# Reordering the second tile of a fused retention and cosine-gated feed-forward kernel, and a k and v load held back in the third

## The chip, the cores and the metric

One core of a Trainium2 chip. The metric is the time of one execution of the kernel on the device, in microseconds (us); the time of a kernel is the median of its runs. The engines: TensorE (PE in the profile, its weight loads PEld), VectorE (DVE), ScalarE (ACT), GpSimd (POOL), and SyncE (SP), which here issues nearly all transfers between HBM and the on-chip memory. Each engine takes its instructions in the order in which the program gives them; waits between engines are semaphores.

## The reference

Retention over 8 batches, 8 heads, 576 positions and 64 features per head, then a feed-forward layer over the 4608 tokens:

```python
scores = scale * np.matmul(q, k.transpose(0, 1, 3, 2))
ret = scores * Dmat                     # gamma[h] ** (i - j) where i >= j, else 0
x = np.matmul(ret, v).transpose(0, 2, 1, 3).reshape(4608, 512)
h = x @ w_in                            # 512 -> 2048
out = (h * np.cos(h)) @ w_out           # 2048 -> 512
```

All inputs and the output are float32; the kernel rounds to bf16 ahead of the matmuls.

## The kernel before

**Blocks and tiles.** The 4608 tokens are 18 token blocks of 256 rows (0 to 17) and nine tiles of 512 tokens (0 to 8). Tile n of the feed-forward layer takes its x from blocks 2n and 2n+1. Retention runs ahead of the feed-forward work: while tile 1 is computed, blocks 3 to 6 are prepared, turned, scored or summed.

**What one block needs.** Its q, k and v are loaded by SP (`load`, L140 and L154). q and k are multiplied by powers of gamma (`scaled`, L203; mostly on POOL, for block 3's q on DVE) and v is rounded (`round_v`, L214, POOL). PE turns q and k (`turned`: 32 transposes, L239, into one PSUM bank or two), and two copies bring them back to SBUF as qkT, one on DVE and one on ACT (L245); where both halves lie in one bank, ACT's copy waits for DVE's. `scores` makes 32 small matmuls (L332), and DVE masks them in two instructions (L341, "ret"). `sums_of` makes the block's state sums (24 or 32 small matmuls, L365, banks "st"); its inner `add` chains them on DVE with the running state (up to four instructions, L412 and L416, "s_all"), and ACT rounds the result (L425, "sb"). `outputs` multiplies ret with v (L449) and the states with q (L477), and ACT copies the result to SBUF as xT (L496).

**The feed-forward half.** `mm1` computes h for a group of 1024 PSUM columns (L525), then a cosine on ACT (L538) and a product on DVE (L539) leave gT. Two cosine buffers alternate. Tile 0 multiplies gT with w_out directly (64 matmuls of 512 columns, L1046, in an order written out by hand, with a list `todo` of retention work at fixed places). From tile 1 on, the second product uses seven smaller products per tile instead of eight (`mm2_seven`, `product`, L640), which need sums of quarters of gT (`g_sum`, L579, on DVE and POOL) and sums of quarters of w_out, computed once (`w_sums`, L557, on DVE, four pieces of eight e's at a time; number 7 is written in place over a quarter of w_out). Sums, copies (L673) and stores (L656) of the results follow.

**Tile 1.** Its h is computed in eight groups of 16 matmuls of 256 columns, here called G0 to G7 (in the code the pairs (1, 0) to (1, 7)). G0 to G3 take the columns of block 2, G4 to G7 those of block 3. Each group fills one PSUM bank, in the order m, a, b, m, b, m, a, b, and a bank comes free when DVE has made the product of the group that filled it before. The table `inside` names what is put into a group: key 2 is the middle of a group, key 4 its end, for these groups of four parts. After G3 the product with number 1 is computed, with `outputs(3, "a")` inside it; G4 waits for the xT that this leaves. After G7 come the products 2, 4, 6, 5, 7 and 3, with `first_scores` ahead of 6 (scores and state sums of blocks 4 and 5, on the banks a, b and m), and the outputs of blocks 4 and 5 ahead of 7 and 3.

**Around the border of tile 0 and tile 1**, PE has in this order: the last output matmuls of tile 0, `outputs(2, "b")`, three more, the turn of block 3 on bank "a", the last one, G0. DVE has: the scaling of block 3's q (L203 two times, waiting for the load of q), the copy of tile 0's second output out of bank "m" (L1056), the copy of block 3's turn (L245), the copy of the fourth output (L1056), a piece of the weight sums 4 (L557), the masks of block 3. G0 writes bank "m".

**Order of transfers.** All loads and stores of tile 2 and of the later tiles are issued by SP in program order. `mm2_seven` makes a store for each quarter result (numbers s 0 to 3); `stored(s)` prepares the next block on POOL (`step`) and loads one further ahead (`load_next`). From tile 3 on some stores and loads are put off into lists (`late`) that run ahead of the products 4 and 3; a gate makes a transfer wait for the output matmul that was recorded last (`tiles["end"]`, L477).

Of the kernel before, what the change touches and what calls it, by code (L numbers as in the profile page):

```python
# [17 lines left out]
def kernel(  # L18
# [28 lines left out]
    last = NT - 1  # L47
# [444 lines left out]
    def outputs(j, bank, guard=None):  # L492
        ps = psum.tile([P, DG, BK], F32, tag=bank, name="ov")
        rest = out_own(j, ps, guard)
        out_carried(j, ps)
        nc.scalar.copy(x_of(j), ps)  # L496
        for run in rest:
            run()
# [47 lines left out]
    def w_sums(x, e0, e1):  # L546
        if x == 7:
            w_sum[x] = w_quarter(0, 1)
        elif x not in w_sum:
            w_sum[x] = consts.tile([P, E2, N2], BF16, tag=f"ws{x}", name=f"ws{x}")  # L550
        a, b = {
            5: lambda: (w_quarter(0, 1), w_quarter(0, 0)),
            6: lambda: (w_quarter(1, 1), w_sum[5]),
            4: lambda: (w_quarter(1, 0), w_sum[6]),
            7: lambda: (w_quarter(1, 1), w_quarter(0, 1)),
        }[x]()
        nc.vector.tensor_tensor(  # L557
            out=w_sum[x][:, e0:e1], in0=a[:, e0:e1], in1=b[:, e0:e1], op=ALU.subtract
        )
# [101 lines left out]
    def mm2_seven(n, at, stored, xs=(1, 2, 6, 4, 7, 5, 3), early=None):  # L661
        pend = []

        def flush():
            while pend:
                pend.pop(0)()

        def add(out_, in0, in1):
            return lambda: nc.vector.tensor_tensor(out=out_, in0=in0, in1=in1, op=ALU.add)  # L669

        def copied(tag, x):
            t = op.tile([P, 2, N2], F32, tag=tag, name="ot")
            held.append(lambda ps=tiles["all", x]: nc.scalar.copy(t, ps))  # L673
            return t

        late = {4: [], 3: []}

        def store(t, r, c, s):
            where = n * W + r * 256, c * N2, (c + 1) * N2, t

            def go():
                if 2 < n < last and s == 0:
                    stored_rows(*where, halves=(0,))
                    late[4].append(lambda: stored_rows(*where, halves=(1,), gate=tiles["end"]))
                    stored(s, late)
                elif 2 < n < last - 1 and s == 1:
                    late[3].append(lambda: stored_rows(*where))
                else:
                    queues = (nc.sync, nc.scalar) if n == last and s else (nc.sync, nc.sync)
                    stored_rows(*where, queues)  # L690
                    stored(s)

            return go

        def copies():
            while held:
                held.pop(0)()

        for x in xs:
            if x not in at:  # L700
                copies()
                flush()
            else:
                if at[x].__name__ in ("nothing", "first_scores", "last_outputs", "turning"):
                    copies()
                at[x](flush, pend)
                copies()
                for run in late.pop(x, ()):
                    run()
            if x == 6 and n > 1:  # L710
                late_sums(n, (3,))
            parts = product(n, x, early)
            if x == 1:
                c11 = copied("a", 1)
                tiles["c11"] = c11
                if n > 1:
                    late_sums(n, (5, 6))
            elif x == 2:
                c11 = tiles["c11"]
                if n == 1:  # L720
                    p2 = copied("d", 2)
                    continue
                pend[:0] = [add(c11, c11, tiles["all", 2]), store(c11, 0, 0, 0)]
            elif x == 6:
                u1 = copied("b", 1)
            elif x == 4:
                c21 = copied("c", 4)
            elif x == 7 and n == 1:
                pend += [
                    add(c21, c21, tiles["all", 1]),  # L730
                    add(c22, c22, tiles["all", 1]),
                    store(c21, 1, 0, 1),
                    store(c22, 1, 1, 2),
                    add(c11, c11, p2),
                    store(c11, 0, 0, 0),
                ]
            elif x == 7:
                c22 = copied("d", 1)
                pend += [add(c21, c21, tiles["all", 1]), store(c21, 1, 0, 1)]
            elif x == 5 and n == 1:  # L740
                c22 = copied("d", 5)
            elif x == 5 and n == last:
                for (j, c0, c1), ps in zip(parts, tiles["o", 5]):
                    pend.append(add(c22[:, j, c0:c1], ps, c22[:, j, c0:c1]))
                pend.append(store(c22, 1, 1, 2))
            elif x == 5:
                pend += [
                    add(c22, c22, tiles["all", 5]),
                    add(u1, u1, tiles["all", 5]),
                    store(c22, 1, 1, 2),  # L750
                ]
            elif n < last:
                pend += [add(u1, u1, tiles["all", 5 if n == 1 else 3]), store(u1, 0, 1, 3)]
                flush()
            else:
                flush()
                copies()
                for (j, c0, c1), ps in zip(parts, tiles["o", 5]):
                    add(u1[:, j, c0:c1], ps, u1[:, j, c0:c1])()
                    if c1 == N2:  # L760
                        stored_rows(
                            n * W + j * P, N2, DM, u1[:, j : j + 1, :], (nc.sync, nc.scalar)
                        )
# [3 lines left out]
    def load_next(**kw):  # L767
        nonlocal loaded
        if loaded < NB:
            load(loaded, **kw)  # L770
            loaded += 1

    def step(then_load=True):

        nonlocal prepared
        if prepared < NB:
            prep(prepared)
            round_v(prepared)
            prepared += 1
            if then_load:  # L780
                load_next()
# [184 lines left out]
    def states_and_scores(j, st_bank, sc_bank):  # L966
        add = sums_of(j, st_bank) if st_bank else None
        masks = scores(j, [sc_bank])
        if add:
            add()()  # L970
        for masked in masks:
            masked()
# [3 lines left out]
    for n in range(NT):  # L976
        blocks = blocks_of.get(n) or [(e + k * E2, 0, W) for e in range(0, E2, 2) for k in range(2)]
        for i, (et, c0, cw) in enumerate(blocks):
            inside = {
                (0, 0): {2: block1_outputs},  # L980
                (1, 0): {2: lambda: w_sums(4, 0, 4), 4: lambda: states_and_scores(3, None, ("n", "st"))},
                (1, 1): {4: lambda: adds.append(sums_of(3, ("n", "st"))())},
                (1, 3): {1: lambda: (adds.pop()(), w_sums(6, 4, E2), w_sums(4, 4, E2))},
                (1, 4): {2: lambda: turned(4, ("st", "a"), (act, vec))},
                (1, 7): {2: lambda: turned(5, "m")},
                (2, 0): {1: lambda: adds.append(sums_of(6, ("n", "st"))())},
                (2, 1): {1: lambda: adds.pop()()},
                (2, 5): {1: lambda: turned(7, ("n", "st"))},
            }.get((n, i), {})
            mm1(n, et, c0, cw, banks_of.get(n, turn_of(n) * 3)[i], inside)  # L990
            if (n, i) == (1, 0):
                step(False)
                load_next()
            if (n, i) == (1, 1):
                step(False)
                for r0, ot in stores[3:] + stores[:3]:
                    stored_rows(r0, 0, DM, ot)
                load_next()
                step()
            if (n, i) == (1, 3):  # L1000
                w_sums(7, 0, 4)
                w_sums(7, 4, E2)
                mm2_seven(1, {}, None, (1,), lambda: outputs(3, "a"))
            if n:
                sums_after(n, i)
            if n == 2 and i in (2, 4):
                for y in range(2):
                    scaled(nc.gpsimd, 8, "q" if i == 2 else "k", y)
            if (n, i) == (2, 6):
                round_v(8)  # L1010
                prepared = 9
                load_next()
                load_next()
        if n == 0:
# [6 lines left out]
                (20, lambda: scaled(nc.vector, 2, "q", 1)),  # L1021
                (42, lambda: turned(2, "ab", (act, vec))),
                (42, lambda: round_v(2)),
                (63, lambda: turned(3, "a", (vec, act))),
                (48, lambda: states_and_scores(2, "a", "b")),
                (49, lambda: prep(3, nc.vector)),
                (60, load_next),
# [146 lines left out]
```

## Time and profile before

| | |
|---|---|
| median of 3 runs | 291.77 us (291.66 to 292.05) |
| the profiled execution | 292.45 us, its span 290.7 us |
| TensorE clock granted | 1.00 |
| PE busy | 283.5 us of the span, DVE 218.9, ACT 170.6, POOL 147.1 |
| chain of work that ended last | PE 86%, DVE 7%, DMA 4%, issue 1% |
| transfers | 42.62 MB, 147 GB/s on average |

The span runs from the first to the last instruction on the core, the execution's own time holds what lies around it as well. In the timelines, a row is a run of like instructions of one engine: start, length, engine, line, operation, output and inputs, count, and in brackets how long the engine sat idle before it and what ended that. The length of a run ends with the modelled end of its last instruction, which for PE lies a little after the moment at which the next one could start. In the table of stretches a row gives a stretch of the span, its length, then busy time and instruction count of PE, PEld, DVE, ACT and POOL, the granted clock, the share of the DMA engines and their GB/s.

### The profile page before, as it was taken

To read this page: it belongs to the slowest core of one execution; us is meant where nothing else is said; L and a number is where in the kernel's file an instruction comes from. 1 tells how busy PE (TensorE), PEld (TensorE's weight loads), DVE (VectorE), ACT (ScalarE), POOL (GpSimd) and SP (SyncE) were. 2 spreads that over 40 slices of the span, in tenths; PEclk is the share of its full clock that TensorE was granted. 3 is DMA by queue.
4 is the path that set the end of the run, shared out by engine and by line. 5 is a ranking of instruction groups with operands and counts; after the bars stand their busy time and mean duration, and the time that the engine had idled before them with its cause. 6 is when DMAs were issued, how large, how long until landed. Compare 5 with 4: busy or idle time off the path is not lost.

```text
span 290.7 us, 10530 instructions
## 1 busy us (share of the span) xinstructions
PE 283.5 (97%) x4336; PEld 190.5 (66%) x4336; DVE 218.9 (75%) x309; ACT 170.6 (59%) x200; POOL 147.1 (51%) x169
## 2 busy tenths in 40 slices
PE   7999999999999999999999999999999999999994
PEld 2664446888854786468746874687458845874584
DVE  5777757998868876796779776986698669745943
ACT  6756216657577745677466737673767476536620
POOL 7940423887986994369235933494338023002400
PEclk9999999999999999999999999999999999999999
DMA  7999999988997999943794189417501130122013
GB/s 225 268 173 205 250 238 237 238 195 207 223 233 188 219 235 217 222 93 79 177 235 96 44 203 239 101 41 186 144 0 38 33 84 0 33 60 59 0 38 108
DMA packets 103853, 42.62 MB, mean 147 GB/s; under 512 B 68480, under 2 KB 103296, under 8 KB 103808
## 3 DMA queue, kind: packets, MB, share of 16 engines
q1 hardware_dynamic: 99104, 37.37, 52.8%
q0 software_dynamic: 4256, 4.19, 9.0%
q8 instruction: 36, 0.59, 0.9%
q10 hardware_dynamic: 448, 0.39, 0.4%
q14 instruction: 9, 0.07, 0.1%
HBM read 36.70 MB, written 9.44 MB: 159 GB/s over the span
## 4 chain that ended last, share of the span: by engine, by line
PE 86%; DVE 7%; DMA 4%; issue 1%; ACT 0%; DVEq 0%; ACTq 0%
PE h L525 40%; PE o L640 34%; PE o L1046 3%; PE tr L239 3%; DMA fq<-in_q_dram 3%; PE ov L449 3%; DVE gT L539 2%; DVE ret L312 1%; PE ov L477 1%; PE sc L332 1%; DMA fk<-in_k_dram 1%; PE st L365 1%; DVE qks L171 1%; DVE w_out_sb L557 1%; DVE ws L557 1%; DVE s_all L416 1%
## 5 line engine op out<-in xcount | busy, mean ns | idle before, releaser
L525 PE MATMUL h<-xT,w_in_sb 128*128 128x512 bf16 (+1 forms) x656 | 127.5, 353 | 0.3 <-DVE qkT L245 0.3
L539 DVE TENSOR_TENSOR gT<-h,cosh 128x1024 bf16<-128x1024 f32 x72 | 87.7, 1221 | 26.5 <-ACT cosh L538 25.4
L538 ACT ACTIVATE cosh<-h,half_pi 128x1024 f32<-128x1024 f32 x72 | 80.1, 1114 | 40.6 <-PE h L525 40.6
L525 PEld LDWEIGHTS <-w_in_sb 128*128 128x128 bf16 x656 | 63.6, 98 | 58.9 <-issue 0.5
L579 POOL TENSOR_TENSOR gs<-gT 128x512 bf16<-128x512 bf16 x30 | 38.1, 1271 | 98.9 <-DVE gT L539 98.2
L640 PEld LDWEIGHTS <-gs 128*128 128x128 bf16 x528 | 49.6, 98 | 5.9
L203 POOL TENSOR_TENSOR qks<-fk,gkc 128x512 bf16<-128x512 f32 x32 | 38.5, 1222 | 5.5 <-DMA fk<-in_k_dram 5.5
L640 PEld LDWEIGHTS <-gT 128*128 128x128 bf16 x384 | 36.6, 98 | 6.1
L669 DVE TENSOR_TENSOR ot<-ot,o 128x512 f32<-128x512 f32 x35 | 23.3, 682 | 20.8 <-ACT ot L673 11.0
L245 ACT COPY qkT<-tr 128x1024 bf16<-128x1024 bf16 x29 | 27.7, 1022 | 12.6 <-PE tr L239 11.0
L203 POOL TENSOR_TENSOR qks<-fq,gq 128x512 bf16<-128x512 f32 x28 | 31.5, 1146 | 4.8 <-DMA fq<-in_q_dram 4.3
L640 PE MATMUL o<-w_out_sb,gs 128*128 128x256 bf16 (+1 forms) x264 | 30.7, 270 | 0.0
L640 PE MATMUL o<-w_out_sb,gT 128*128 128x256 bf16 x256 | 30.6, 273 | 0.0
L640 PE MATMUL o<-ws,gs 128*128 128x256 bf16 (+1 forms) x264 | 30.4, 269 | 0.0
L673 ACT COPY ot<-o 128x512 f32<-128x512 f32 x33 | 19.2, 585 | 18.2 <-PE o L640 18.2
L341 DVE TENSOR_TENSOR ret<-sc,mask_c 128x512 bf16<-128x512 f32 x32 | 20.6, 683 | 7.0 <-PE sc L332 7.0
L214 POOL CAST vb<-fv 128x512 bf16<-128x512 f32 x35 | 21.4, 637 | 6.7 <-DMA fv<-in_v_dram 6.5
L425 ACT CAST sb<-s_all 128x768 bf16<-128x768 f32 (+2 forms) x17 | 15.6, 919 | 14.4 <-DVE s_all L416 14.4
L416 DVE TENSOR_TENSOR s_all<-st,s_all 128x256 f32<-128x256 f32 x49 | 20.7, 422 | 1.9 <-PE st L365 0.6
L496 ACT CAST xT<-ov 128x1024 bf16<-128x1024 f32 x16 | 16.2, 1012 | 8.3 <-PE ov L477 8.0
L579 DVE TENSOR_TENSOR gs<-gT 128x512 bf16<-128x512 bf16 (+1 forms) x24 | 16.0, 665 | 0.5
L640 PE MATMUL o<-ws,gT 128*128 128x256 bf16 x128 | 15.3, 273 | 0.0
(83 smaller groups left out, 212.1 us busy)
## 6 DMA issues: line engine op xcount, KB each, us to landing
out_dram<-ot SPq DMA_DIRECT2D x68, 128.0 KB, 2.5
fk<-in_k_dram SPq DMA_DIRECT2D x28, 256.0 KB, 5.3
fv<-in_v_dram SPq DMA_DIRECT2D x28, 256.0 KB, 4.1
fq<-in_q_dram SPq DMA_DIRECT2D x12, 512.0 KB, 5.2
w_out_sb<-in_moe_w_out_dram POOLq DMA_DIRECT2D x4, 512.0 KB, 9.7
fq<-in_q_dram SPq DMA_DIRECT2D x4, 384.0 KB, 5.9
fk<-in_k_dram SPq DMA_DIRECT2D x2, 512.0 KB, 6.0
fv<-in_v_dram SPq DMA_DIRECT2D x2, 512.0 KB, 5.9
```

The costliest lines, as they stand in the source:

```text
L203: return eng.tensor_tensor(out=dst.rearrange("p b a d -> p a b d"), in0=src.rearrange("p (a b) d -> p a b d", a=2), in1=by.rearrange("p (a ...
L214: runs[y](vb[:, y], f[:, :, y, :] if j < NP_B else f[:, y])
L245: lambda r=r: evacs[r](tiles["qkT", j][:, :, :, :, r * HP : r * HP + HP], pss[r])
L341: nc.vector.tensor_tensor(out=ret[:, he].rearrange("p b y i -> p (b y) i"), in0=ps[he].rearrange("p b y i -> p (b y) i"), in1=mask_c.unsqu ...
L416: nc.vector.tensor_tensor(out=s32[:, u], in0=ps[c.half][:, c.y], in1=s32[:, u - 1] if u else tiles["run"], op=ALU.add,)
L525: nc.tensor.matmul(ps[:, j, :], lhsT=w_in_sb[:, dg, (et + j) * P : (et + j + 1) * P], rhs=xT[:, dg, c0 : c0 + w], start=dg == 0 and not (i ...
L538: nc.scalar.activation(cosh, ps, ACTF.Sin, bias=half_pi, scale=1.0)
L539: nc.vector.tensor_mul(gT[:, et : et + m, c0 : c0 + w], ps, cosh)
L579: i = eng.tensor_tensor(out=tiles["gs", n, x][:, e : e + step], in0=a[:, e : e + step], in1=b[:, e : e + step], op=op_,)
L640: nc.tensor.matmul(dst[i], lhsT=lhs[:, e, j * P : (j + 1) * P], rhs=rhs[:, e, c0:c1], start=(fresh and e == 0 and (i == 0 or len(parts) > 2)),
L669: return lambda: nc.vector.tensor_tensor(out=out_, in0=in0, in1=in1, op=ALU.add)
L673: held.append(lambda ps=tiles["all", x]: nc.scalar.copy(t, ps))
```

## The change

No instruction is added or taken away on PE, DVE, ACT or POOL; they are put in another order, and two stores and a load change places on SP.

- Block 3's turn leaves the end of tile 0 and goes into the middle of G0, on bank "b" instead of "a". Its state sums go from the end of G1 to the end of G0, its scores from the end of G0 to the middle of G2. On DVE the copies of tile 0's outputs now stand together ahead of the copy of the turn, and the state additions ahead of the products of G0 and G1, the masks behind them.
- The two pieces of the weight sums 7 stood behind G3's product, ahead of DVE's copy of block 4's turn. Now the first piece stands behind this copy, and the second behind G5's product.
- In tile 2, the store with number 0 prepares a block and loads only q of the next (block 11); its k and v are put off to the place ahead of product 3, gated on the output matmul recorded last. There they stand behind the two stores of number 2, which come from product 5. The store with number 1 is put off in tile 2 as well, as it was from tile 3 on.

```diff
@@ mm2_seven, store @@
-                elif 2 < n < last - 1 and s == 1:
+                elif n == 2 and s == 0:
+                    stored_rows(*where)
+                    step(False)
+                    load(loaded, "q")
+                    late[3].append(lambda: load_next(names="kv", gate=tiles["end"]))
+                elif 1 < n < last - 1 and s == 1:
                     late[3].append(lambda: stored_rows(*where))
@@ the table inside @@
-                (1, 0): {2: lambda: w_sums(4, 0, 4), 4: lambda: states_and_scores(3, None, ("n", "st"))},
-                (1, 1): {4: lambda: adds.append(sums_of(3, ("n", "st"))())},
+                (1, 0): {
+                    2: lambda: (turned(3, "b", (vec, act)), w_sums(4, 0, 4)),
+                    4: lambda: adds.append(sums_of(3, ("n", "st"))()),
+                },
+                (1, 2): {2: lambda: states_and_scores(3, None, ("n", "st"))},
                 (1, 3): {1: lambda: (adds.pop()(), w_sums(6, 4, E2), w_sums(4, 4, E2))},
-                (1, 4): {2: lambda: turned(4, ("st", "a"), (act, vec))},
+                (1, 4): {2: lambda: (turned(4, ("st", "a"), (act, vec)), w_sums(7, 0, 4))},
@@ after a group @@
             if (n, i) == (1, 3):
-                w_sums(7, 0, 4)
+                mm2_seven(1, {}, None, (1,), lambda: outputs(3, "a"))
+            if (n, i) == (1, 5):
                 w_sums(7, 4, E2)
-                mm2_seven(1, {}, None, (1,), lambda: outputs(3, "a"))
@@ the list todo of tile 0 @@
-                (63, lambda: turned(3, "a", (vec, act))),
```

## The prediction

> **What bounds the kernel now.** I read the page's busy table first, then the table of stretches, then the chain of work that ended last, then each engine's timeline from 45 to 82 us, where the change lies.
>
> ```profile
> PE 283.5 (97%) x4336; PEld 190.5 (66%) x4336; DVE 218.9 (75%) x309; ACT 170.6 (59%) x200; POOL 147.1 (51%) x169
> ```
> ```profile
> 45.00:63.18 18.18, 17.22 (x353) 13.86 (x349) 16.64 (x22) 11.13 (x12) 12.77 (x14) 1.00 0.99 236
> 63.18:82.00 18.82, 18.67 (x434) 15.88 (x434) 16.41 (x24) 12.45 (x18) 15.46 (x15) 1.00 0.82 200
> 82.00:112.00 30.00, 30.00 (x530) 20.12 (x529) 23.70 (x32) 19.73 (x24) 25.70 (x27) 1.00 0.89 219
> ```
>
> First pair in each row: length, TensorE (PE) busy. From 82 us on PE has no hole until the tail, so whatever PE gains or loses before 82 us comes out whole at the end, and work moved after 82 us is free as long as PE does not have to wait for it. In 45 to 63.18 VectorE (DVE) is busy 16.64 of 18.18 us. Here are PE's two holes:
>
> ```profile
> 45.57 0.82 PE L1046 MATMUL o<-w_out_sb,gT 128*128 128x512 bf16 x3
> 46.49 0.29 PE L239 MATMUL tr<-ident,qks 64*128 64x64 bf16 x8
> 47.09 0.52 PE L239 MATMUL tr<-ident,qks 64*128 64x64 bf16 x24 [0.31 <-DVE qks L203]
> 47.55 0.39 PE L1046 MATMUL o<-w_out_sb,gT 128*128 128x512 bf16 x1
> ```
> ```profile
> 59.47 0.64 PE L239 MATMUL tr<-ident,qks 64*128 64x64 bf16 x32
> 60.04 2.79 PE L525 MATMUL h<-xT,w_in_sb 128*128 128x256 bf16 x24
> 63.18 0.49 PE L525 MATMUL h<-xT,w_in_sb 128*128 128x256 bf16 x3 [0.34 <-DVE qkT L245]
> ```
>
> A row ends about 0.16 after PE could take the next instruction (one matmul's latency over its pace). So hole one is 46.23 to 46.49 and 46.63 to 47.09, 0.72 in all: block 3's transposes wait for its q, scaled by DVE. Hole two: 24 matmuls at 0.109 (3.50 us for the 32 from 52.22) are done at 62.67; G6 starts at 63.18, 0.51 late, since its bank "a" waits for DVE's copy of block 4's turn. 1.23 us is all that can be won.
>
> **Part 1: block 3's turn into the middle of G0.** Hole one seems to go. But these rows decide what is late next:
>
> ```profile
> 45.74 1.29 DVE L203 TENSOR_TENSOR qks<-fq,gq 128x512 bf16<-128x512 f32 x2 [1.33 <-DMA fq<-in_q_dram]
> 46.95 0.68 DVE L1056 COPY ot<-o 128x512 f32<-128x512 f32 x1
> 47.66 0.69 DVE L245 COPY qkT<-tr 128x1024 bf16<-128x1024 bf16 x1
> ```
>
> G0 writes bank "m", which tile 0 still holds until DVE has copied its second output (L1056). That copy stands behind the same q scaling on DVE, and ends at 47.63. The built changed kernel keeps both the order on DVE and the wait of G0's first weight load on DVE. So G0 starts at 47.69 plus 0.03 instead of 47.77 (0.05 gained), PE now idle from 46.45, and the 32 transposes, which lay in that shadow, come after: 0.57 (59.47 to 60.04, the same 32 in the same place of a group). Sum: **+0.50**. Bounds: 0, if q lands 1.3 us earlier, so that the copy is over by 46.45; +0.57, if nothing is gained. I take the middle row, this trace's. State sums (32, 0.38) and scores (32, 0.38) only change places between groups: three interruptions of h before and after, nothing for PE.
>
> Does the new order hold block 3 up? G0's 16 take 1.84 with their switch (47.77 to 49.61), so turn ends 49.21, G0 50.13, sums 50.51, G1 52.3, scores 53.6, G2 54.5, G3 56.3. DVE: copy of the turn to 49.93, weight sum 0.6 to 50.54, four state adds 1.78 (chain) to 52.41, two gT products at 1.13 to 54.67, masks 1.19 to 55.86. The output matmuls that need the masks come at 56.75 (+0.50 on 56.25): 0.9 spare, else they would pay. ScalarE rounds the states (1.0) between the cosines of G2 and G3, to 56.7; needed at 57.3. xT of block 3 is ready near 58.85, G4 takes it at 59.0: 0.15 spare. Cost 0.
>
> **Part 2: block 4's copies ahead of the weight sums of 7.** DVE's two L557 before the copy cost 2.77; now the copy follows G3's product, ends near 61.3, and bank "a" is wanted at 63.17. Hole two goes: **-0.51**, so G6 starts where it does today. Bounds: -0.51, the whole hole; 0, if G3's product slips past 61.4 and G5 waits for bank "m" instead (I get 60.4 to 61.4).
>
> **Part 3: the weight sums that were put off.** The second half now stands behind G5's product, beside GpSimd (POOL).
>
> ```profile
> 67.20 1.04 POOL L203 TENSOR_TENSOR qks<-fk,gkc 128x512 bf16<-128x512 f32 x1
> ```
> ```profile
> 67.41 1.37 DVE L579 TENSOR_TENSOR gs<-gs,gT 128x1024 bf16<-128x1024 bf16 x1
> 69.55 1.22 DVE L539 TENSOR_TENSOR gT<-h,cosh 128x1024 bf16<-128x1024 f32 x1 [0.76 <-ACT cosh L538]
> 70.81 0.69 DVE L579 TENSOR_TENSOR gs<-gT 128x1024 bf16<-128x1024 bf16 x1
> ```
>
> The first L579 takes 1.37 and the one without POOL work 0.69: it sits until POOL's instruction ends at 68.20, then needs 0.58; POOL's next then takes 1.49 for 1.04. I use that: DVE waits for POOL's running instruction, then 0.6; then POOL 1.0. G5's product is tied to its cosine and ends at 65.66 (today 65.39). Then: put-off sum, POOL's q instruction ends 65.75, to 66.37; first L579, POOL's next ends 67.33, to 67.9; G6's product 1.14 to 69.1; second L579, POOL's to 69.9, to 70.5; G7's product to 71.65, today 70.77. The 0.76 of DVE idle ahead of it, today's cover, is used up. G7's bank "b" is wanted for block 4's state sums:
>
> ```profile
> 71.21 0.92 PE L365 MATMUL st<-vb,qks 64*64 64x64 bf16 x56
> ```
>
> They start at 71.21 today; block 5's, behind them, wait for a ScalarE copy until 71.68. At 71.78 plus 0.30 for 24 sums, block 5's start at 72.08: **+0.40**. Bounds: 0, where POOL is never in the way (each 0.6: product over at 69.8, cosine ready 69.52); +1.2, where each of the three meets a whole POOL instruction (1.53, the longest L557: product over at 72.5, block 5's sums at 72.9).
>
> Here the Trainium skill speaks against the change ("SBUF — State Buffer", Who interferes with whom): a VectorE instruction with two SBUF inputs and a GpSimd one that reads SBUF exclude each other, the later waiting for the whole of the other. The 1.37 and 1.49 agree with it. Were it not so, and each instruction kept today's own duration (1.39, 0.91, 1.37), the product would end at 71.6, near the same; with free ports the term would be 0 and the time 291.8.
>
> **Part 4: k and v of block 11 held back** until an output matmul at 110.9, behind two stores. SP issues k at 109.03 today, v at 111.11 to 113.9; I expect k from 112, v to 118, landing (median 6.2 for k, 4.0 for v) by 123. POOL takes them at 136.98 and 138.97. What is queued behind on SP, two pairs of stores and block 12's q, has as much room: block 12 is scaled after 158. **0**; bounds 0 and 0.5 (a late prep would first eat 14 us).
>
> **Sum**: +0.50 - 0.51 + 0.40 + 0 = +0.39. The profiled execution took 292.45 (span 290.7 and 1.75 around it), so 292.84 by its own scale; the median of the runs, 291.77, is 0.68 lower: 292.16, say **292.2**.
>
> **Rivals.**
> - *Port backlog* (slower). G7's product ends past 72.0, because POOL's q or k of block 6 land so that each of three L557/L579 meets a full instruction; part 3 is 1.0, and the masks of block 5, over 0.57 ahead of their use at 78.62 today, come level. Sum +1.0 to +1.2: 292.9. For: 1.42 and 1.53 stand in the trace. Against: 0.91 does too. It decides from G7's product at 72.0 on. Chance 0.30.
> - *q lands early* in runs without the profiler: part 1 near 0, part 3 small: 291.4. Against: DMA queues near full from 30 to 60 us. Chance 0.13.
> - *Both holes go* (faster): G0 is not held by the copy, -0.72 - 0.51: 290.5. Against: the copy's row. Chance 0.07.
> - *It doesn't do what it says*: G5 waits for G3's product as long as G6 did for the copy; +0.50 + 0 + 0.40: 292.7. Chance 0.05.
>
> **How the numbers follow.** Forecast 0.45, its own range 291.8 to 292.5. Range 291.3 to 293.0. Within 0.2% (0.58 us, about what a measurement here can tell from no change): the forecast but for 0.10 above 292.35, and 0.10 of early q: 0.45. Slower: 0.10 + 0.30 + 0.05. Faster: 0.07 + 0.03.
>
> **What would show it.** Part 1: no wait of tr on L203, G0's first matmul at 47.7, PE idle over a us before it; wrong if G0 starts near 46.5. Part 2: no gap ahead of G6. Part 3: block 4's sums wait for G7's product, tile 2's first matmul near 82.3 instead of 81.71. Part 4: no wait of POOL on DMA near 137. A gap after 82 us would break the argument.

## The result and the profile after

The changed kernel took 292.51 us in the median of 22 runs (291.78 to 294.50), the kernel before, run beside it, 292.07 us in 22 runs. The ratio is 1.0026 (95% interval 1.0014 to 1.0038): slower by a quarter of a per cent. The profiled execution took 292.23 us, its span is 290.5 us. It is one of the shorter runs of the changed kernel, while the profile of before (292.45 us) was one of the longer runs of its kernel. The two profiles by themselves therefore point the wrong way, and the medians and the experiments have to decide.

First the busy table, the chain of work that ended last, and the stretches of the changed kernel (columns as before: length, then PE, PEld, DVE, ACT and POOL busy, clock, DMA):

```profile
PE 283.8 (98%) x4336; PEld 190.8 (66%) x4336; DVE 219.0 (75%) x309; ACT 170.5 (59%) x200; POOL 147.2 (51%) x169
...
PE 89%; DMA 4%; DVE 2%; POOL 1%; ACT 1%; issue 0%; SPq 0%; ACTq 0%
```
```profile
45.00:63.18 18.18, 17.80 (x370) 14.37 (x367) 16.22 (x21) 11.34 (x12) 13.10 (x14) 1.00 1.03 239
63.18:82.00 18.82, 18.42 (x431) 15.41 (x429) 17.20 (x25) 12.48 (x18) 15.50 (x14) 1.00 0.88 216
82.00:112.00 30.00, 30.00 (x531) 20.20 (x530) 23.71 (x33) 19.63 (x23) 25.88 (x27) 1.00 0.84 202
```

DVE's share of the chain fell from 7% to 2%. In the first stretch PE is busy 0.58 us more than before, so the holes there are nearly gone; in the second it is busy 0.25 less, so something new waits there. From 82 us on PE is dense again. The places, in PE's timeline of the changed kernel:

```profile
45.73 1.04 PE L1053 MATMUL o<-w_out_sb,gT 128*128 128x512 bf16 x4
46.95 1.03 PE L525 MATMUL h<-xT,w_in_sb 128*128 128x256 bf16 x8 [0.18 <-ACT xT L496]
47.92 0.64 PE L239 MATMUL tr<-ident,qks 64*128 64x64 bf16 x32
...
59.90 5.41 PE L525 MATMUL h<-xT,w_in_sb 128*128 128x256 bf16 x48
...
70.89 0.69 PE L365 MATMUL st<-vb,qks 64*64 64x64 bf16 x56 [0.15 <-DVE gT L539]
...
75.93 0.72 PE L477 MATMUL ov<-qkT,sb 64*64 64x64 bf16 x24
```

There is no wait of the transposes on q, and the 48 matmuls from 59.90 run through G6 without a gap: both holes of before are gone. In their place block 4's state sums wait for a product (0.15), as part 3 of the forecast said. The L477 row takes 0.72 where before took 0.36. The weight loads of its last two matmuls come late, and the profile names no releaser ("issue"):

```profile
76.44 0.11 PEld L477 LDWEIGHTS <-sb 64*64 64x64 bf16 x2 [0.26 <-issue]
```

DVE, the same execution:

```profile
44.74 1.29 DVE L203 TENSOR_TENSOR qks<-fq,gq 128x512 bf16<-128x512 f32 x2 [0.17 <-DMA fq<-in_q_dram]
45.95 0.68 DVE L1063 COPY ot<-o 128x512 f32<-128x512 f32 x1
```

Block 3's q came 1.00 us earlier than in the profile of before (44.74 against 45.74). So the copy out of bank m was done in time, and G0 waited for the xT of block 2 instead. Whether q's landing or the change took the first hole away cannot be told from two profiles.

**A measure by stages.** PE's path from `outputs(2)` (L449 near 44.8) to tile 2's first h holds the same PE instructions in every kernel of this study. I cut it at three starts and took the differences from PE's timeline: A, to product 1 (L640 near 55.6: block 3's turn and G0 to G3); B, on to block 5's scores (L332 near 70.3: G4 to G7, products 2 and 4); C, on to product 6 (the state sums of blocks 4 and 5); D, on to tile 2's first h. What remains to the end of the span is 208.8 to 209.3 us in all fourteen profiles; the two profiles of before alone differ by 0.28 of this, so no later gain or loss can be told. The start of A lies between 44.66 and 45.38 us, a spread that this measure leaves out. "q" is when DVE began to scale block 3's q, counted from the start of A; in the kernels named copy_first that comes behind the copy and is not the time at which q landed.

| kernel (one profile each) | q | A | B | C | D | sum |
|---|---|---|---|---|---|---|
| before, first profile | 1.03 | 11.01 | 15.22 | 1.12 | 9.65 | 37.00 |
| before_again | 0.18 | 10.36 | 14.71 | 1.13 | 9.65 | 35.85 |
| loads_only | 0.10 | 10.36 | 14.71 | 1.12 | 9.65 | 35.84 |
| sums_only | 0.31 | 10.36 | 14.70 | 1.97 | 9.74 | 36.77 |
| sums_both | 0.60 | 10.58 | 14.76 | 1.12 | 9.70 | 36.16 |
| after | -0.13 | 10.71 | 14.70 | 1.23 | 10.02 | 36.66 |
| turn_only | 0.48 | 11.07 | 15.34 | 1.13 | 10.71 | 38.25 |
| early7 | 0.67 | 11.25 | 14.71 | 1.12 | 9.66 | 36.74 |
| q_first | -0.38 | 11.51 | 14.71 | 1.12 | 10.05 | 37.39 |
| copy_first | 0.50 | 10.71 | 14.70 | 1.40 | 9.74 | 36.55 |
| early7_copy_first | 0.88 | 10.71 | 14.70 | 1.13 | 9.65 | 36.19 |
| q_first_copy_first | 0.50 | 10.71 | 14.71 | 1.45 | 9.74 | 36.61 |
| copy_first_sums_both | 0.53 | 10.70 | 14.71 | 1.13 | 9.74 | 36.28 |
| q_first_early7_before | -0.13 | 11.55 | 14.71 | 1.12 | 9.98 | 37.36 |

### The profile page after: what moved, and what is told of

The parts are those of the page before. It is cut to its first block, busy times and chain, and to the rows that moved or that the text cites. A ratio compares the mean times of both kernels' runs of the same rounds, so it can differ in the third digit from the quotient of the medians.

```text
span 290.5 us, 10527 instructions
## 1 busy us (share of the span) xinstructions
PE 283.8 (98%) x4336; PEld 190.8 (66%) x4336; DVE 219.0 (75%) x309; ACT 170.5 (59%) x200; POOL 147.2 (51%) x169
## 4 chain that ended last, share of the span: by engine, by line
PE 89%; DMA 4%; DVE 2%; POOL 1%; ACT 1%; issue 0%; SPq 0%; ACTq 0%
PE h L525 42%; PE o L640 33%; PE o L1053 5%; PE tr L239 3%; PE ov L449 2%; DMA w_in_sb<-in_moe_w_in_dram 2%; DMA fv<-in_v_dram 2%; PE sc L332 2%; PE ov L477 1%; PE st L365 1%; DVE gT L539 1%; DVE gs L579 1%; POOL qks L203 1%; DVE w_out_sb L557 0%; ACT cosh L538 0%
## 5 line engine op out<-in xcount | busy, mean ns | idle before, releaser
L579 POOL TENSOR_TENSOR gs<-gT 128x512 bf16<-128x512 bf16 x30 | 38.1, 1271 | 98.6 <-DVE gT L539 97.9
L640 PEld LDWEIGHTS <-gs 128*128 128x128 bf16 x528 | 49.6, 98 | 6.0
L640 PEld LDWEIGHTS <-gT 128*128 128x128 bf16 x384 | 36.6, 98 | 6.1
L640 PE MATMUL o<-w_out_sb,gs 128*128 128x256 bf16 (+1 forms) x264 | 30.7, 270 | 0.0
L640 PE MATMUL o<-w_out_sb,gT 128*128 128x256 bf16 x256 | 30.6, 273 | 0.0
L640 PE MATMUL o<-ws,gs 128*128 128x256 bf16 (+1 forms) x264 | 30.4, 269 | 0.0
L579 DVE TENSOR_TENSOR gs<-gT 128x512 bf16<-128x512 bf16 (+1 forms) x24 | 16.6, 690 | 0.5
L640 PE MATMUL o<-ws,gT 128*128 128x256 bf16 x128 | 15.3, 273 | 0.0
```

The lines of the kernel that those rows point to most:

```text
L579: i = eng.tensor_tensor(out=tiles["gs", n, x][:, e : e + step], in0=a[:, e : e + step], in1=b[:, e : e + step], op=op_,)
L640: nc.tensor.matmul(dst[i], lhsT=lhs[:, e, j * P : (j + 1) * P], rhs=rhs[:, e, c0:c1], start=(fresh and e == 0 and (i == 0 or len(parts) > 2)),
```

## The experiments

All were timed in five rounds beside the kernel before (12 runs each, but 11 of q_first and 6 of q_first_early7_before), except before_again, which is one profile.

**The three parts alone.** turn_only is the kernel before with part 1, sums_only with parts 2 and 3, loads_only with part 4; their diffs are the matching hunks of the change. For instance sums_only against before:

```diff
-                (1, 4): {2: lambda: turned(4, ("st", "a"), (act, vec))},
+                (1, 4): {2: lambda: (turned(4, ("st", "a"), (act, vec)), w_sums(7, 0, 4))},
...
-                w_sums(7, 0, 4)
-                w_sums(7, 4, E2)
                 mm2_seven(1, {}, None, (1,), lambda: outputs(3, "a"))
+            if (n, i) == (1, 5):
+                w_sums(7, 4, E2)
```

> The kernel before with part 1 alone (block 3's turn, state sums and scores moved; weight sums 7 and loads as before). Theory (bank m's copy behind the q scaling): G0 starts no earlier than before unless q lands early, so the 32 transposes cost up to 0.5 us, and DVE, about 0.4 us later at G3's product and still with two weight sums ahead of block 4's copy, makes the hole ahead of G6 longer than 0.51 us: together +0.5 to +1.0 us against before. Rival (the loss sits in the held-back load): within 0.15 us of before. Rival (the loss sits in the weight sums put off): at or below before.

Measured: 292.67 us, ratio 1.0031 (1.0010 to 1.0051). Part 1 alone is slower, within the intervals by as much as the whole change. PE of turn_only:

```profile
47.25 1.05 PE L525 MATMUL h<-xT,w_in_sb 128*128 128x256 bf16 x8 [0.53 <-DVE ot L1058]
...
63.47 2.78 PE L525 MATMUL h<-xT,w_in_sb 128*128 128x256 bf16 x24 [0.47 <-DVE qkT L245]
...
77.46 0.22 PE L477 MATMUL ov<-qkT,sb 64*64 64x64 bf16 x2 [0.33 <-issue]
```

G0 waits for the copy out of bank m (L1058 here), as forecast, and the hole ahead of G6 is still there because part 2 is missing. A third loss, in stage D, has no releaser in the profile; its first stall stands ahead of the same two matmuls as in the changed kernel.

> The kernel before with part 2 and 3 alone (weight sums 7 behind block 4's copy and behind G5's product). Theory: the hole ahead of G6 goes (-0.51 us), and the wait of block 4's state sums for G7's product gives back 0 to 0.4 us: -0.5 to 0 us. Rival (the weight sums put off are the loss): +0.4 us or more, with a wait of state sums on G7's product of 0.9 us.

Measured: 292.25 us, ratio 1.0002 (0.9985 to 1.0018). The next two fences are PE and DVE of sums_only:

```profile
59.39 5.41 PE L525 MATMUL h<-xT,w_in_sb 128*128 128x256 bf16 x48
...
71.12 0.69 PE L365 MATMUL st<-vb,qks 64*64 64x64 bf16 x56 [0.89 <-DVE gT L539]
```
```profile
64.51 1.52 DVE L557 TENSOR_TENSOR w_out_sb<-w_out_sb 128x1024 bf16<-128x1024 bf16 x1
65.96 1.52 DVE L579 TENSOR_TENSOR gs<-gT 128x1024 bf16<-128x1024 bf16 x1
...
68.54 1.39 DVE L579 TENSOR_TENSOR gs<-gs,gT 128x1024 bf16<-128x1024 bf16 x1
69.86 1.21 DVE L539 TENSOR_TENSOR gT<-h,cosh 128x1024 bf16<-128x1024 f32 x1
```

There is no gap ahead of G6, and PE waits 0.89 us for G7's product. The put-off L557 and both L579 ahead of that product each take 1.39 to 1.52 us, where one undisturbed L579 takes 0.69; POOL scales q and k beside them without a break from 64.45 to 69.39. So in this profile part 3 gives back what part 2 can win, on the path that was forecast.

> The kernel before with part 4 alone (k and v of block 11 gated, two pairs of stores ahead of or behind them). Theory: 0 within 0.15 us, no wait of POOL or PE after 105 us. Rival (the held-back load is the loss): +0.4 us, with a PE gap or a longer tail after 105 us.

Measured: 291.97 us, ratio 0.9994 (0.9980 to 1.0009). Part 4 is worth nothing that can be measured; in the changed kernel too, k of block 11 leaves at 111.57, v at 114.68 to 117.05, and POOL waits for no transfer near 137 us. Added up, the three ratios give 0.31 + 0.02 - 0.06 = 0.27%, beside 0.26% for the whole, though each has an interval of some 0.15 to 0.2% on either side.

**The copy ahead of q.** copy_first is the changed kernel with DVE's scaling of block 3's q moved behind its copy out of bank m:

```diff
-                (49, lambda: prep(3, nc.vector)),
+                (56, lambda: prep(3, nc.vector)),
```

> The changed kernel with block 3's q scaling (and the k scaling recorded with it) recorded after DVE's copy out of bank m instead of ahead of it. Theory: G0 no longer waits for q and starts when xT of block 2 is there, near 46.8 us, 0.9 us earlier than where q is late; against the changed kernel -0.3 to -0.9 us on the median and fewer long runs, against before -0.4 us. Rivals (loss in the load or in the weight sums): as the changed kernel, +0.4 us against before.

Measured: 292.23 us, ratio 1.0007 (0.9991 to 1.0022). DVE, then PE of copy_first:

```profile
44.81 0.69 DVE L1063 COPY ot<-o 128x512 f32<-128x512 f32 x1 [0.19 <-ACT ot L1063]
45.42 1.28 DVE L203 TENSOR_TENSOR qks<-fq,gq 128x512 bf16<-128x512 f32 x2
```
```profile
47.00 1.03 PE L525 MATMUL h<-xT,w_in_sb 128*128 128x256 bf16 x8 [0.18 <-ACT xT L496]
```

The copy no longer stands behind a wait for a load, and G0 starts when xT is there. Stage A is 10.70 or 10.71 in all four kernels with this edit, though DVE began the scaling between 0.50 and 0.88 us into the stage and took 1.28 to 2.20 us for it. In none of the four did DVE wait for q, so a later landing was not met. In the four kernels with block 3's turn in G0 and the copy behind q it is 10.71, 11.07, 11.25 and 11.51. Against the changed kernel's 1.0026, which was timed in another series, the time is some 0.5 us shorter, as expected; against before, the expected -0.4 us did not come, and the interval still holds a part of the loss.

**The weight sums 7 out of the way.** early7 is the changed kernel with both pieces made in tile 0; early7_copy_first joins it with copy_first:

```diff
-                    (2, 5, 0), (8, 5, 4), (19, 6, 0),
+                    (2, 5, 0), (8, 5, 4), (19, 6, 0), (48, 7, 0), (62, 7, 4),
```

> The changed kernel with the weight sums 7 computed in tile 0 (first piece behind block 2's masks, second behind block 3's q scaling), so that no L557 of 7 stands behind G3 to G5. Theory (block 4's state sums wait for G7's product behind a DVE queue blocked by POOL): that wait is gone, -0.2 to -0.5 us against the changed kernel, 0 to +0.3 against before; the cost of part 1 stays where q is late. Rival (part 1 is the whole loss): as the changed kernel, +0.4 us or more against before.

> The changed kernel with the weight sums 7 in tile 0 and the copy out of bank m ahead of block 3's q scaling. Theory: both terms go, the gain of the hole ahead of G6 stays: -0.3 to -0.6 us against before. Rival (something else in part 1, such as the transposes inside G0 as such, costs): 0 to +0.4 us.

Measured: early7 292.47 us, 1.0022 (1.0008 to 1.0036); with the copy first as well 292.00 us, 0.9997 (0.9984 to 1.0010). In both, stage C is at its floor (1.12 and 1.13), so the put-off sums are what G7's product waited behind. By its time, though, early7 lies where the changed kernel does (1.0026), as the rival said: what stage C costs is too small to show there, and most of the loss is part 1's. early7 keeps the copy behind q, and G0 starts at 47.54 after 0.71 us of waiting for it. With both costs removed the kernel is level with before, not ahead of it; stage A is still 10.71 against 10.36 in before_again, which is the rival's cost of the transposes inside G0.

**q loaded ahead of k.** q_first is the changed kernel with block 3's load order turned from k, q, v to q, k, v. q_first_copy_first adds copy_first. q_first_early7_before is the kernel before with that order and both pieces of the weight sums 7 made earlier, in tile 0 and in G0:

```diff
-    load_next(names="kqv", gate=w_dma[8])
+    load_next(names="qkv", gate=w_dma[8])
```

> The changed kernel with the transfers of block 3 issued in the order q, k, v instead of k, q, v. Theory (part 1 costs because the copy out of bank m stands behind a q that comes late): q lands some 2 us earlier, G0 starts when xT of block 2 is there (near 46.9 us) in every run, -0.3 to -0.6 us against the changed kernel, and fewer long runs. Rival (the transposes inside G0 or the wait for G7's product are the loss): as the changed kernel, +0.4 us against before.

> The changed kernel with block 3 loaded in the order q, k, v and the copy out of bank m ahead of the q scaling. In the q-first kernel DVE's two q scalings took 2.60 us beside POOL's k scaling, and G0 still waited 0.97 us for the copy. Theory (what costs is the copy's place behind the scaling, whatever makes the scaling end late): G0 starts when xT of block 2 is there, near 46.9 us, -0.4 to -0.6 us against the q-first kernel. Rival (the transposes inside G0, or k landing later, are the loss): as the q-first kernel, +0.7 us against before.

> The kernel before with two edits of its own: block 3 loaded in the order q, k, v, and the weight sums 7 computed in tile 0 and in the middle of G0. Theory: the first hole (0.72 us, transposes waiting for the q scaling) and the second (0.51 us, G6 waiting for a copy behind two L557) both go and nothing is put in their place: -0.7 to -1.2 us against before, the fastest of all. Rival (the holes are replaced by the next wait, k of block 3 or a DMA later on): within 0.3 us of before.

Measured: q_first 292.78 us, 1.0026 (1.0015 to 1.0037); q_first_copy_first 292.26 us, 1.0005 (0.9982 to 1.0027); q_first_early7_before 293.41 us, 1.0049 (1.0033 to 1.0064). The gain I expected of an early q did not come, and the kernel before with this order and early sums is the slowest of all. With the copy first as well, the wait and most of the loss of q_first are gone, as expected. DVE and POOL of q_first show why:

```profile
44.29 2.60 DVE L203 TENSOR_TENSOR qks<-fq,gq 128x512 bf16<-128x512 f32 x2
46.80 1.28 DVE L1063 COPY ot<-o 128x512 f32<-128x512 f32 x2
```
```profile
43.85 1.04 POOL L203 TENSOR_TENSOR qks<-fk,gkc 128x512 bf16<-128x512 f32 x1 [3.97 <-DMA fk<-in_k_dram]
45.12 1.21 POOL L203 TENSOR_TENSOR qks<-fk,gkc 128x512 bf16<-128x512 f32 x1 [0.24 <-DMA fk<-in_k_dram]
```

q is there as soon as DVE wants it, but k is now landing at the same moment, and DVE's two scalings sit out both of POOL's: they take 1.15 and 1.53 us, which fits one held until 44.89, when POOL's first ends, and the other until 46.33, when its second does. They take 2.60 us together against 1.29 alone. The copy ends later than with a late q, and G0 waits 0.97 us for it. In q_first_early7_before the pair takes 2.99 us and PE's transposes wait 1.01 us for it. The Trainium skill ("SBUF — State Buffer", Who interferes with whom) says that a VectorE instruction with two SBUF inputs and a GpSimd one that reads SBUF exclude each other for whole instructions; these rows agree.

**The weight sums behind the turn's copy.** sums_both is the kernel before with both pieces right behind DVE's copy of block 4's turn; copy_first_sums_both is the changed kernel with the copy first and the same place for the sums:

```diff
-                (1, 4): {2: lambda: turned(4, ("st", "a"), (act, vec))},
+                (1, 4): {2: lambda: (turned(4, ("st", "a"), (act, vec)), w_sums(7, 0, 4), w_sums(7, 4, E2))},
```

> The kernel before with both weight sums 7 right behind DVE's copy of block 4's turn (middle of G4), none of them put off behind G5. Theory (the hole ahead of G6 is the copy behind two L557; the put-off second piece is what makes G7's product late): no hole ahead of G6 and no wait of block 4's sums for G7's product, -0.2 to -0.5 us against before and against the sums-only kernel. Rival (the wait for G7's product comes from POOL's meeting with the two L579 alone, wherever the L557 stand): as the sums-only kernel, 0 against before, with a wait of 0.3 to 0.9 us on G7's product.

> The changed kernel with the copy out of bank m ahead of the q scaling and both weight sums 7 right behind the copy of block 4's turn. Theory: neither the wait of G0 for the copy nor that of block 4's sums for G7's product is left: -0.5 to -0.8 us against the changed kernel, -0.1 to -0.4 us against before. Rival (block 3's turn inside G0 costs by itself): 0 to +0.3 us against before.

Measured: sums_both 292.26 us, 1.0002 (0.9979 to 1.0026); copy_first_sums_both 292.13 us, 0.9994 (0.9974 to 1.0015). Neither has a gap ahead of G6 or a wait of the state sums (B 14.76 and 14.71, C 1.12 and 1.13), yet neither is shown to beat the kernel before. Their intervals reach 0.2% to each side, some 0.6 us, so a gain as large as one hole could hide in them. But it may also be that the holes are not in every run of before; so the kernel before was profiled a second time.

**The kernel before, once more.**

> The kernel before once more, for a second look at its holes. Theory (the holes ahead of block 3's turn and of G6 depend on when q of block 3 lands and on how the L557 meet POOL): holes between 0 and 0.8 us each, smaller where DVE starts the q scaling before 45 us, and the run shorter by what they lack. Rival (the holes are fixed by the order): 0.7 and 0.5 us again, whatever q does.

Measured: 291.58 us, span 289.9. PE, then DVE:

```profile
46.40 0.64 PE L239 MATMUL tr<-ident,qks 64*128 64x64 bf16 x32
46.97 0.39 PE L1046 MATMUL o<-w_out_sb,gT 128*128 128x512 bf16 x1
47.20 1.91 PE L525 MATMUL h<-xT,w_in_sb 128*128 128x256 bf16 x16
...
59.46 5.41 PE L525 MATMUL h<-xT,w_in_sb 128*128 128x256 bf16 x48
```
```profile
44.96 1.29 DVE L203 TENSOR_TENSOR qks<-fq,gq 128x512 bf16<-128x512 f32 x2 [0.47 <-DMA fq<-in_q_dram]
...
55.91 1.41 DVE L557 TENSOR_TENSOR ws<-w_out_sb,ws 128x1024 bf16<-128x1024 bf16 x2
```

The same kernel has neither hole. q landed 0.78 us earlier, and the transposes run without a wait. The pair of L557 ahead of G3's product took 1.41 us. DVE, then POOL in the first profile of before:

```profile
56.49 2.13 DVE L557 TENSOR_TENSOR ws<-w_out_sb,ws 128x1024 bf16<-128x1024 bf16 x2
```
```profile
57.01 2.52 POOL L203 TENSOR_TENSOR qks<-fq,gq 128x512 bf16<-128x512 f32 x2 [0.49 <-PE ov L449]
```

There the pair took 2.13 and lay beside POOL's scaling from 57.01 on. That is 0.72 us more on DVE, and hole two was 0.51. So each hole hung on a moment: when q landed, and whether POOL was at work beside that pair. The second may hang on the first. Counted from the start of A, the pair began at 11.13 in before_again and loads_only, which have no hole ahead of G6, and at 11.78 and 11.98 in the first profile of before and in turn_only, which have it; the late q had held PE, and with it DVE, back by then. No run isolates this.

How often a run of before has the holes is not known. The run without them (291.58 us) is 0.54 us shorter than the median of the 29 runs beside it (292.12), and the run with both (292.45) is longer than the median of 292.07: the usual run lies between the two.

## Why the prediction came out as it did

The forecast was 292.2 us and +0.39 on the profiled execution; measured were 292.51 us, and +0.44 by the medians or 0.0026 of 292.07, that is +0.76, by the ratio. The time lies in the range, just past the top of the forecast's own part of it (292.5), and the sign is that of the sum; "within 0.2%" and "slower" had been given 0.45 each, and the ratio falls to "slower". Of the 0.3 us between 292.2 and 292.51, nearly all is the base: the sum started from a median of 291.77, and the kernel before took 292.07 beside the changed one. That the sum itself came out close is in part luck, since part 2 and part 3 differ from run to run by as much as their size.

- **Part 1, +0.50, bounds 0 and +0.57: the mechanism held, the lower bound failed.** Stage A gives the term at equal landing of q. Before takes 10.36 with q at up to 0.31, 10.58 at 0.60 and 11.01 at 1.03: it grows one for one from about 0.38 on. The changed order takes 10.71 at -0.13, 11.07 at 0.48 and 11.25 at 0.67: it grows from about 0.13 on. The term is thus +0.35 with an early q and about +0.60 with a late one, where the forecast had +0.50 (its own 0.57 less 0.05 is 0.52). The step that failed is "0, if q lands 1.3 us earlier". G0 also needs block 2's xT, 2.08 us after the start of A in the changed kernel; the transposes of before ran inside that wait (G0 at 2.42 in before_again), and now come after it (2.08 + 0.57 = 2.65), which is 0.23. The other 0.12 is one interruption of h more than before: the 64 matmuls of G0 to G3 take 0.97 + 0.98 + 2.73 + 2.63 = 7.31 in the changed kernel and 1.84 + 1.85 + 3.50 = 7.19 in before. The forecast had put that at nothing: it counted three interruptions of h before and after, but before has two (scores and state sums). This is also why +0.60 lies over the upper bound. Hole one was read too long: only the rows of 512 columns end some 0.16 after the next instruction can start, the rows of transposes 0.07 (59.47 plus 0.64 against 60.04). It is 0.65, as stage A says (11.01 against 10.36), and not 0.72. "G0's first matmul at 47.7, PE idle over a us before it" was wrong for the profiled execution, where q was early.
- **Part 2, -0.51: right where the hole exists, too large for runs without it.** Stage B is 14.70 in the changed kernel. It was 15.22 in the first profile of before, 15.34 in turn_only, but 14.71 in the two others with this part's order of before, before_again and loads_only. The step that failed is the base, "0.51 late", read from one execution.
- **Part 3, +0.40, bounds 0 and +1.2: right in mechanism, the size within its bounds.** Stage C rose from 1.12 to 1.23 in the changed kernel, 1.40 in copy_first, 1.45 in q_first_copy_first, 1.97 in sums_only: +0.11 to +0.85. The five kernels with both pieces moved elsewhere have none of it (1.12 or 1.13). In q_first C is 1.12 as well: there PE is so late from stage A (0.80 over after) that it no longer has to wait for the product.
- **Part 4, 0: right** (loads_only).
- **Rivals.** *q lands early* happened in the changed kernel's profile and was no gain, for the reason under part 1. *Both holes go* was true of that profile as well: it is 0.22 us shorter than the profile of before, but 0.65 longer than before_again, which has no holes to lose. *Port backlog* is near to what sums_only shows (G7's product ends at 71.07, ahead of the 72.0 that was named, but PE is ahead too and waits 0.89), so it is a matter of the run more than a case of its own. *It doesn't do what it says* is out: G5 waits for nothing.

**In one sentence:** the change pays 0.35 us in and around G0 when q is early and 0.60 when it is late, and in most profiles some 0.1 to 0.9 ahead of block 4's state sums, and it wins the second hole, 0.5 us, which the kernel before has only in some runs; the first hole, where it exists, only turns into G0's wait for the copy behind the same scaling.

**What stays open.** Stage D is 9.65 in both profiles of before, and 10.02, 10.71 and 10.05 in after, turn_only and q_first. In these three the weight loads of the same two matmuls, the last of the first 24 L477 of the stage, come late after "issue" (0.26, 0.45 and 0.30 us), and in turn_only two of the last product as well (0.62); no other profile has that. These stalls are as large as the terms argued about here, and no run isolates them. In q_first_early7_before (9.98) the weight loads of a product wait 0.42 for POOL's sums, and 0.17 to 0.19 in the four profiles with 9.74. The runs of over 292.8 us are 24 of 57 in the four kernels with the turn in G0 and the copy behind q, 5 of 48 in the four with the copy first, and 14 of 114 of before. That fits the copy's wait for a late q, but no long run was profiled next to a short one of the same changed kernel, so it is argued, not shown. No kernel here is shown to beat the one before.

## What to carry to other kernels

Before a hole is counted as a gain, profile the same kernel twice: a hole that hangs on a load's landing or on two engines' instructions meeting may be missing from many runs, while the price of removing it can be paid in all of them. When work is moved out of a hole, ask what else ended there: here the transposes filled a wait for another input (xT), and moving them left that wait empty. On an in-order engine, a copy that frees a PSUM bank should not stand behind an instruction that waits for a transfer; putting the copy first left stage A at 10.70 or 10.71 us in all four profiles, where it had spread from 10.71 to 11.51.

## What the runs showed of the hardware that was not expected

An earlier transfer made its consumer slower: with q ahead of k, DVE's two scalings took 2.60 and 2.99 us instead of 1.29, where POOL's scalings of k ran beside them. And of two executions of the same kernel, one had 1.15 us more on PE's path between 44.8 and 81.7 us than the other (37.00 against 35.85), all of it in stages A and B.
